# A kernel's own scheduler learns of eight shared transfer places, keeps five input loads under way, and starts the first expert weights later

## The chip, the cores and the metric

The kernel runs on one core of a Trainium2 chip. The core has five engines, each with a queue of instructions of its own that it takes in order: TensorE (PE; its weight loads are shown apart as PEld), VectorE (DVE), ScalarE (ACT), GpSimd (POOL) and SyncE (SP), which here only issues transfers. Transfers are issued by SP, ACT and POOL and carried by 16 DMA engines. The metric is the device time of one execution in microseconds, and less is better; the median over runs counts.

## The reference

Decayed causal attention without a softmax (a retention layer) over 8 batches, 8 heads, 576 positions and a head size of 64, and then a mixture of 8 experts over the 4608 rows of 512 that come out of it. Each row goes to the two experts with the highest noisy logits.

```python
def _attn_ref(q, k, v):
    scores = np.matmul(q, k.transpose(0, 1, 3, 2)) / np.sqrt(D_)
    gamma = 1.0 - 2.0 ** (-5.0 - np.arange(H))
    Dmat = np.where(rel >= 0, gamma[:, None, None] ** rel, 0.0)     # rel: row - column
    return np.matmul(scores * Dmat, v)

def _moe_ref(x, w_gate, w_noise, noise, w1, w2):
    logits = x @ w_gate + np.log1p(np.exp(x @ w_noise)) * noise
    top2 = np.argpartition(-logits, 2, axis=1)[:, :2]               # and their softmax: top2_w
    for e in range(8):
        for k in range(2):
            mask = top2[:, k] == e
            h = np.maximum(x[mask] @ w1[e], 0.0)                    # 512 to 1024
            out[mask] += top2_w[mask, k, None] * (h @ w2[e])        # 1024 to 512
```

q, k and v are 28.3 MB in float32, the experts' weights 33.6 MB.

## The kernel before

The kernel is written as a list of operations, and a scheduler of its own, `Plan`, decides in which order they are issued. An operation names the engines that may do it with an estimated cost for each, the buffers that it reads and writes, a priority (`prio`, less is sooner) and, where it is a transfer, an estimated transfer time (`dma`). `Plan.run` keeps a model clock: of all operations whose predecessors are placed and whose buffers can be had, it places the one that can start soonest (then the lowest priority), books its engine, and sets its end (`fin`). A transfer ends when its queue's transfer time is through and 2.0 us more have gone (`DMA_LAT`). When all are placed, the instructions are issued in that order. So the estimates make the order of each engine's queue, and no more than that: the waits in the finished program come from the tiles that instructions touch and from the transfers' semaphores. For these the finished program has eight places that the transfers of SP and ACT share, taken in turn in the order of issue, and eight more for those of POOL; a transfer waits until the one that had its place before, eight transfers earlier, has landed. The model of before knows nothing of these places. An `after` argument is a predecessor in the model alone.

What the operations are:

- The attention runs in 16 units (`unit`): four batch pairs, two halves of the heads, two batches each. `load` issues five SP transfers for each unit: k and v in two halves (L390, 0.25 MB each) and q (L385, 0.5 MB), into ten float32 buffers `big`. `load_tail` (L401) brings the last 64 positions of a batch pair in six transfers. `cast` makes bf16 of them: k on ACT or DVE (L420, L422), q and v on DVE or POOL with the decay multiplied in (L428, L435; the tail's on POOL, L578). `tr` transposes K and Q on TensorE (L453), `scores` multiplies them (L478) and DVE evicts with the mask (L486), `states` makes the running state (L509), evicted by L252 (ACT) or L254 (DVE), and `out_` the output (L541 within a chunk, L551 across), evicted into `xT`. `tail` does the same for the tail (L587, L600, L618, L622).
- After each batch pair `route` computes the logits (L652) and a long chain of small DVE and POOL steps on them (L660 to L763), which gives the ranks (L716, L718) and the table of rows (L769, two groups of nine matrix multiplications), and puts the rows back by token (L793), copied to `xr` and stored to `xd` in DRAM by five ACT transfers (L802). The four routings end where the second group of L769 ends.
- `weights` of experts 0, 1 and 2 are cast by POOL transfers, four for each expert: two for w1 (L859) and two for w2 (L863). `record` lets them follow, in the model, the landing of the loads of the units in `WAIT`: 8, 11 and 14. The weights of the experts 3 to 7 come later, by SP into `big` (L873, L876).
- The experts work on tiles of 128 rows in pairs. `fetch` gathers the rows (L913 on POOL, from `xd`), transposes them (L922), `up` multiplies by w1 (L979, 32 for a full pair, in four groups of 8), evicted with the relu (L993, L995), `down` by w2 (L1014, 8 for each tile), and `finish` stores first results to `yd` (L1067 on SP) or adds the earlier result, gathered by L1042, and scatters to `out` (L1075 on POOL). Fifteen tiles, in nine pairs, of the experts 0, 1 and 2 can be done while the attention still runs, as the first three routings close them; all others follow the last routing.

TensorE's queue thus mixes attention, routing and early expert tiles in the order of the model clock until about 202 us, and from there on has expert tiles alone.

Of the kernel before, what the change touches and what calls it, by code (L numbers as in the profile page):

```python
# [27 lines left out]
NH = E * HPE  # L28
FIRST = (1216, 1019, 855, 690, 526, 361, 197, 0)
YOFF = [sum(min(-(-x // P) * P, CAP) for x in FIRST[:e]) for e in range(E + 1)]  # L30
WAIT = (8, 11, 14)
CLOSE = ((256, 0, 0, 0, 0, 0, 0, 0), (512, 384, 384, 0, 0, 0, 0, 0), (768, 640, 512, 0, 0, 0, 0, 0))
PLW = 8
XW = DM // 2 + PLW
# [19 lines left out]
class Plan:  # L54
# [55 lines left out]
    def run(self):  # L110
        free, dma_free = {}, {}
        head = {k: 0 for k in self.fifo}
        used = {}
        ready = [o for o in self.ops if not o.need]
        order = []

        def slot(b, taken):
            s = self.slots[b.cls]
            lim = self.quota[b.cls].get(b.stream, len(s))
            if lim < len(s) and all(head[k] >= len(v) for k, v in self.fifo.items()  # L120
                                    if k[0] == b.cls and k[1] != b.stream):
                lim = len(s)
            if used.get((b.cls, b.stream), 0) + sum(t[1].n for t in taken if t[1].cls == b.cls) + b.n > lim:
                return None
            ok = lambda x: x[1] is None and all(x is not y for t in taken for y in t[0])
            best = None
            for i, x in enumerate(s):
                if b.n == 2:
                    if i % 2 or not (ok(x) and ok(s[i + 1])):
                        continue  # L130
                    c, k = [x, s[i + 1]], (max(x[0], s[i + 1][0]), 0)
                elif not ok(x):
                    continue
                else:
                    c, k = [x], (x[0] + (0.3 if len(s) == 8 and ok(s[i ^ 1]) else 0.0), 1)
                if best is None or k < best[0]:
                    best = k, c
            return best and best[1]

        while ready:  # L140
            pick = None
            for o in ready:
                taken = []
                ok = all(b.cls is None or b.t is not None or b in o.allocs for b in o.bufs)
                if not ok:
                    continue
                for n, b in enumerate(o.allocs):
                    k = (b.cls, b.stream)
                    q = self.fifo[k]
                    m = len([t for t in taken if (t[1].cls, t[1].stream) == k])  # L150
                    if q[head[k] + m] is not b:
                        ok = False
                        break
                    x = slot(b, taken)
                    if x is None:
                        ok = False
                        break
                    taken.append((x, b))
                if not ok:
                    continue  # L160
                t0 = max([y[0] for x, b in taken for y in x], default=0.0)
                best = None
                for e, c in o.eng.items():
                    t = max(t0, free.get(e, 0.0))
                    for p in o.preds:
                        t = max(t, p.fin + (0.0 if p.on == e and not p.dma else self.LAT))
                    x = t + c + (self.BIAS.get(e, 0.0) if len(o.eng) > 1 else 0.0)
                    if best is None or x < best[0]:
                        best = x, e, t, c
                _, e, t, c = best  # L170
                key = (round(t * 20), o.prio, o.i)
                if pick is None or key < pick[0]:
                    pick = (key, o, e, t, c, taken)
            if pick is None:
                raise RuntimeError("no operation can go on: " + str([(o.i, o.prio) for o in ready[:20]]))
            _, o, e, t, c, taken = pick
            ready.remove(o)
            o.on = e
            free[e] = t + c
            o.fin = t + c  # L180
            if o.dma:
                x = max(dma_free.get(e, 0.0), t + c)
                if e == "SP":
                    x += o.dma / 0.95
                else:
                    x += o.dma / 0.5
                    if dma_free.get("SP", 0.0) > t + c:
                        dma_free["SP"] += o.dma
                dma_free[e] = x
                o.fin = dma_free[e] + self.DMA_LAT  # L190
            for x, b in taken:
                for y in x:
                    y[1] = b
                b.t = x[0][2] if b.n == 1 else x[0][3]
                k = (b.cls, b.stream)
                head[k] += 1
                used[k] = used.get(k, 0) + b.n
            for b in o.bufs:
                if b.cls is None:
                    continue  # L200
                b.left -= 1
                if not b.left:
                    for x in self.slots[b.cls]:
                        if x[1] is b:
                            x[1] = None
# [12 lines left out]

class Kernel:
# [154 lines left out]
    def unit(u):  # L374
        return u // 4, u // 2 % 2, u % 2

    def load(self, u):
        pl, nc = self.pl, self.nc
        bp, hq, b = self.unit(u)
        d = self.u[u] = {}  # L380
        for n in "kqv":
            t = d["raw" + n] = pl.buf("big", "att")
            s = self.src[n][2 * bp + b, 4 * hq:4 * hq + 4]
            if n == "q":
                pl.op("SP", 0.07, lambda e, s=s, t=t: nc.sync.dma_start(  # L385
                    out=t.t.rearrange("p (h x) -> p h x", h=4), in_=s[:, :512].rearrange("h (p r) d -> p h (r d)", r=4)),
                    w=[t], prio=u, dma=1.6)
            else:
                for c in range(2):
                    pl.op("SP", 0.07, lambda e, s=s, t=t, c=c: nc.sync.dma_start(  # L390
                        out=t.t.rearrange("p (c h x) -> p c h x", c=2, h=4)[:, c],
                        in_=s[:, 256 * c:256 * c + 256].rearrange("h (p r) d -> p h (r d)", r=2)),
                        w=[(t, c)], prio=u, dma=0.96)

    def load_tail(self, bp, prio):
        pl, nc = self.pl, self.nc
        d = self.tails[bp] = {}
        for n in "kqv":
            t = d["raw" + n] = pl.buf("half", "tl")
            for b in range(2):  # L400
                pl.op("SP", 0.07, lambda e, n=n, t=t, b=b: nc.sync.dma_start(  # L401
                    out=t.t[b * HD:(b + 1) * HD].rearrange("p (h d) -> p h d", h=E),
                    in_=self.src[n][2 * bp + b, :, 512:, :].rearrange("h s d -> s h d")),
                    w=[(t, b)], prio=prio, dma=0.8)

    def cast(self, u):
        pl, nc = self.pl, self.nc
# [676 lines left out]

    def record(self):
        pl = self.pl
        self.u, self.tails, self.T, self.xT, self.W, self.t, self.keep, self.scats, self.wdma = {}, {}, {}, {}, {}, {}, {}, {}, []
        self.setup()
        for u in range(3):
            self.load(u)  # L1090
# [39 lines left out]
        for i, t in enumerate(ts[:ne]):  # L1130
# [6 lines left out]
            for fp in range(4):  # L1137
                r, w, c = g.deps(fp)
# [4 lines left out]
        for i in range(ne, len(ts) + 1):  # L1143
# [7 lines left out]
            if i < len(ts):  # L1151
                e = ts[i][0]
# [3 lines left out]
            else:  # L1156
                e, po, hT = ts[-1][0], self.t[i - 1]["po"], self.t[i - 1]["hT"]
# [168 lines left out]
```

## Time and profile before

| | us |
|---|---|
| median of three runs (522.32, 524.5, 525.01) | 524.5 |
| the profiled execution | 519.78 |
| its span, first to last instruction | 518.2 |
| TensorE busy | 435.5 (84%) |
| GpSimd busy | 298.2 (58%) |
| VectorE busy | 222.4 (43%) |
| ScalarE busy | 209.7 (40%) |

The page of the profile cuts the span in 40 equal slices of 13 us and gives the busy share of each in tenths. Here TensorE, the clock that it was granted, and the DMA engines:

```profile
PE   1887639876798899899999889989997799988993
...
PEclk9999757987969579999999999999999799999998
DMA  8999999999765314427679864885865333444333
```

In the first ten slices the DMA engines are full; TensorE is far from full in the first, in the sixth, and by turns up to the sixteenth, where the clock is low in places too. From the seventeenth slice on TensorE is nearly always busy. In these digits a 9 is 90% or more; a busy TensorE is not one at its peak, since multiplications overlap.

Transfers by queue: q1 is SP's, q10 ACT's, q0 POOL's.

```profile
q1 hardware_dynamic: 71874, 60.36, 38.7%
q0 software_dynamic: 15264, 36.89, 26.8%
q10 hardware_dynamic: 4928, 4.87, 2.8%
```

The columns are packets, MB, and the time that the packets took as a share of 16 engines over the span.

### The profile page before, as it was taken

The page shows a single profiled execution, that of the slowest core. Times are in us where ns is not written, and L with a number is a line of the kernel's source. Part 1 is how long each engine was busy: PE and PEld are TensorE (multiplying, and loading weights), DVE is VectorE, ACT ScalarE, POOL GpSimd, SP SyncE. Part 2 cuts the span into 40 slices and gives each one's busy share as a digit, 9 for nine tenths or more (in the row PEclk, how much of TensorE's full clock was granted, in tenths as well). Part 3 has the DMA queues.
Part 4 walks back from the last instruction along what each step waited for, and adds up shares of the span by engine and source line. Part 5 has one row for each costly group of instructions (what it writes and reads, how often), then busy time and mean ns, then how long its engine had stood idle before and what let it go on. Part 6 is the DMA issues. An engine that isn't in the chain of part 4 may idle for free.

```text
span 518.2 us, 12025 instructions
## 1 busy us (share of the span) xinstructions
PE 435.5 (84%) x4784; PEld 296.4 (57%) x4784; DVE 222.4 (43%) x535; ACT 209.7 (40%) x345; POOL 298.2 (58%) x355
## 2 busy tenths in 40 slices
PE   1887639876798899899999889989997799988993
PEld 1665527664576666567565546645645465654661
DVE  2465597793649359411515152341251121312132
ACT  3465425753565454345435334342441222322311
POOL 8846794795677527513253555546447366666453
PEclk9999757987969579999999999999999799999998
DMA  8999999999765314427679864885865333444333
GB/s 242 226 273 231 310 277 267 295 274 294 162 138 99 109 60 143 146 76 246 250 247 372 280 199 134 297 281 162 281 256 175 104 127 120 146 162 132 124 123 104
DMA packets 92125, 102.91 MB, mean 199 GB/s; under 512 B 21502, under 2 KB 70143, under 8 KB 92066
## 3 DMA queue, kind: packets, MB, share of 16 engines
q1 hardware_dynamic: 71874, 60.36, 38.7%
q0 software_dynamic: 15264, 36.89, 26.8%
q10 hardware_dynamic: 4928, 4.87, 2.8%
q8 instruction: 38, 0.62, 0.5%
q14 instruction: 21, 0.17, 0.1%
HBM read 83.20 MB, written 26.63 MB: 212 GB/s over the span
## 4 chain that ended last, share of the span: by engine, by line
PE 46%; issue 15%; POOL 11%; DMA 11%; DVE 7%; SPq 4%; ACT 3%; another core or an unknown queue 1%; POOLq 0%; ACTq 0%; DVEq 0%
PE ps L1014 15%; PE ps L979 14%; DMA xg<-xd,xi 4%; PE ps L509 4%; POOL xg L913 3%; DMA out_dram<-half,xg 3%; POOL half L1042 2%; DMA half<-in_q_dram 2%; PE ps L922 2%; PE ps L453 2%; PE ps L541 2%; PE ps L478 2%; POOL out_dram L1075 2%; SPq L390 2%; DMA big<-in_k_dram 1%
## 5 line engine op out<-in xcount | busy, mean ns | idle before, releaser
L979 PE MATMUL ps<-half,W 128*128 128x256 bf16 (+2 forms) x1344 | 221.2, 264 | 10.2 <-issue 6.1
L1014 PE MATMUL ps<-W,half 128*128 128x512 bf16 x624 | 222.7, 387 | 3.3 <-issue 1.8
L979 PEld LDWEIGHTS <-W 128*128 128x128 bf16 x1344 | 122.4, 98 | 79.9 <-issue 24.1
L993 ACT ACTIVATE half<-ps 128x512 bf16<-128x512 f32 (+2 forms) x160 | 87.1, 558 | 174.2 <-PE ps L979 108.8
L913 POOL DMA_INDIRECT xg<-xd,xi x80 | 83.2, 1040 | 104.9 <-DMA out_dram<-half,xg 24.9
L1014 PEld LDWEIGHTS <-half 128*128 128x128 bf16 x624 | 61.6, 100 | 34.0 <-issue 17.5
L1075 POOL DMA_INDIRECT out_dram<-half,xg x39 | 39.2, 1006 | 33.2 <-DVE half L1071 16.9
L1071 DVE SCALAR_TENSOR_TENSOR half<-ps,xg,half 128x512 f32<-128x512 f32 (+1 forms) x39 | 27.7, 745 | 68.0 <-issue 24.2
L1042 POOL DMA_INDIRECT half<-yd,xg x39 | 39.1, 1002 | 11.9 <-issue 11.6
L486 DVE TENSOR_TENSOR half<-ps,mask 128x512 bf16<-128x512 f32 x64 | 40.2, 708 | 6.5 <-ACT half L1061 3.2
L254 DVE COPY half<-ps 128x1024 bf16<-128x1024 bf16 (+2 forms) x47 | 30.9, 661 | 22.1 <-PE ps L922 8.7
L252 ACT ACTIVATE half<-ps 128x1024 bf16<-128x1024 bf16 (+2 forms) x31 | 29.4, 969 | 24.6 <-POOL oh L763 7.2
L428 POOL TENSOR_TENSOR half<-big,tab 128x1024 bf16<-128x1024 f32 x15 | 29.5, 1964 | 14.8 <-PE ps L551 5.9
L922 PE MATMUL ps<-ident__69,xg 128*128 128x128 bf16 (+1 forms) x320 | 28.7, 225 | 8.7 <-DMA xg<-xd,xi 7.4
L509 PE MATMUL ps<-half,half 64*64 64x64 bf16 (+2 forms) x512 | 32.4, 239 | 2.5 <-issue 1.9
L453 PE MATMUL ps<-ident__69,half 128*128 128x128 bf16 x256 | 24.9, 271 | 9.0 <-ACT half L420 6.0
L922 PEld LDWEIGHTS <-xg 128*128 128x128 bf16 (+1 forms) x320 | 21.4, 102 | 18.2 <-DMA xg<-xd,xi 10.0
L435 POOL TENSOR_TENSOR half<-big,tab 128x512 bf16<-128x512 f32 x26 | 28.4, 1106 | 0.5 <-issue 0.5
L509 PEld LDWEIGHTS <-half 128*64 128x64 bf16 (+1 forms) x512 | 20.1, 117 | 15.0 <-issue 7.2
L252 ACT ACTIVATE tb<-ps 64x512 bf16<-64x512 f32 x30 | 17.7, 591 | 26.4 <-PE ps L509 12.6
L1063 DVE TENSOR_SCALAR half<-ps,xg 128x512 f32<-128x512 f32 x9 | 6.8, 750 | 49.6 <-issue 32.7
L453 PEld LDWEIGHTS <-half 128*128 128x128 bf16 x256 | 21.3, 126 | 10.0 <-ACT half L420 6.0
(173 smaller groups left out, 436.9 us busy)
## 6 DMA issues: line engine op xcount, KB each, us to landing
big<-in_moe_w_dram SPq DMA_DIRECT2D x40, 512.0 KB
yd<-half SPq DMA_DIRECT2D x40, 256.0 KB
big<-in_k_dram SPq DMA_DIRECT2D x32, 256.0 KB
big<-in_q_dram SPq DMA_DIRECT2D x16, 512.0 KB
big<-in_v_dram SPq DMA_DIRECT2D x32, 256.0 KB
W<-in_moe_w_dram POOLq DMA_DIRECT2D x12, 512.0 KB
xd<-xr ACTq DMA_DIRECT2D x16, 264.0 KB
xg<-xd,xi POOLq DMA_INDIRECT x80
```

What stands on the lines that cost most here:

```text
L252: self.nc.scalar.activation(out, in_, Act.Copy)
L254: self.eng(e).tensor_copy(out, in_)
L453: nc.tensor.transpose(v[:, hp, x, :], i[:, y, hp * P:(hp + 1) * P], ident.t)
L486: nc.vector.tensor_tensor(S.t.bitcast(BF16).rearrange("p (h c x) -> p h c x", h=2, c=2)[:, h], p[h].t.rearrange("p (c x) -> p c x", c=2), ...
L509: nc.tensor.matmul(o[h * HD:(h + 1) * HD, hp, n, :], lhsT=kv[0][:k, r, c, 2 * hp + h, :], rhs=m, start=(hp == 0 and c == 0 and k == P and ...
L913: pl.op("POOL", 1.3, lambda _, x=x, h=h, n=n: nc.gpsimd.indirect_dma_start(out=x.t[:n, :], out_offset=None, in_=self.xd[:rows, :], in_offs ...
L922: nc.tensor.transpose(pv()[:, di, s * P:s * P + n], xb[:, di * P:(di + 1) * P], ident.t[:n, :n])
L979: nc.tensor.matmul(pv()[:, f2, :], lhsT=w.t[:, o:o + P], rhs=xv()[:, di, :n], start=(di == 0), stop=(di == KD - 1))
L993: nc.scalar.activation(hv(), pv(), Act.Relu)
L1014: nc.tensor.matmul(po[s].t[:n], lhsT=hv[:, s * P:s * P + n], rhs=w.t[:, o:o + DM], start=(f == 0), stop=(f == KF - 1))
L1042: pl.op("POOL", 1.3, lambda _, b=b, iy=iy, n=self.size(j): nc.gpsimd.indirect_dma_start(out=b.t[:n, :], out_offset=None, in_=self.yd[:rows ...
L1075: ins = nc.gpsimd.indirect_dma_start(out=self.out[:, :], out_offset=IOff(ap=io()[:n], axis=0), in_=o.t[:n, :], in_offset=None, bounds_chec ...
```

## The change

Three things are changed. First, `Plan.run` keeps for each of the two groups of queues (SP and ACT together, POOL) the list of ends of the transfers placed so far, and lets a new transfer start no sooner than the end of the one eight before it. Second, every load of q, k and v, the tails' too, goes through a new function `inp`, which makes it follow, in the model, the fifth load before it, so that five are under way. Third, `WAIT` is (11, 14, 15) instead of (8, 11, 14). No operation is added or taken away; what each computes is the same.

```diff
-WAIT = (8, 11, 14)
+WAIT = (11, 14, 15)
...
         used = {}
+        lanes = {"SP": [], "POOL": []}
+        lanes["ACT"] = lanes["SP"]
...
                     t = max(t0, free.get(e, 0.0))
+                    if o.dma and len(lanes[e]) >= 8:
+                        t = max(t, lanes[e][-8])
...
                 o.fin = dma_free[e] + self.DMA_LAT
+                lanes[e].append(o.fin)
...
+    def inp(self, fn, t, prio, dma):
+
+        self.inps.append(self.pl.op("SP", 0.07, fn, w=[t], prio=prio, dma=dma, after=self.inps[-5:-4]))
+
     def load(self, u):
...
             if n == "q":
-                pl.op("SP", 0.07, lambda e, s=s, t=t: nc.sync.dma_start(
+                self.inp(lambda e, s=s, t=t: nc.sync.dma_start(
...
-                    w=[t], prio=u, dma=1.6)
+                    t, u, 1.6)
...
     def load_tail(self, bp, prio):
...
-                pl.op("SP", 0.07, lambda e, n=n, t=t, b=b: nc.sync.dma_start(
+                self.inp(lambda e, n=n, t=t, b=b: nc.sync.dma_start(
...
-                    w=[(t, b)], prio=prio, dma=0.8)
+                    (t, b), prio, 0.8)
```

The two halves of k and v in `load` are changed in the same way (0.96 each), and `record` starts with an empty list `inps`.

In the finished program the order of all five queues is different. On SP the tails' loads stand later: those of the first batch pair behind unit 4's instead of before unit 3's, those of the second behind unit 8's instead of between unit 6's k and q, those of the third behind unit 12's instead of between unit 10's q and v. On POOL the first w1 transfers of expert 0 stand behind unit 11's casts, those of expert 1 behind unit 14's, and those of expert 2 behind the last L763 of the third routing. On TensorE the first L979 stands behind the second L769 group of the second routing instead of ahead of the first. Some operations that two engines may do change sides: DVE does 4 L254, 3 L422 and 3 L435 less, ACT 4 L252 and 3 L420 more, POOL 3 L435 more. The lines of the changed kernel are 4 to 9 higher than those named here.

More of the change, by code (lines that the diff above doesn't have):

```diff
@@ L384, in load @@
             if n == "q":
-                pl.op("SP", 0.07, lambda e, s=s, t=t: nc.sync.dma_start(
+                self.inp(lambda e, s=s, t=t: nc.sync.dma_start(
                     out=t.t.rearrange("p (h x) -> p h x", h=4), in_=s[:, :512].rearrange("h (p r) d -> p h (r d)", r=4)),
-                    w=[t], prio=u, dma=1.6)
+                    t, u, 1.6)
             else:
                 for c in range(2):
-                    pl.op("SP", 0.07, lambda e, s=s, t=t, c=c: nc.sync.dma_start(
+                    self.inp(lambda e, s=s, t=t, c=c: nc.sync.dma_start(
                         out=t.t.rearrange("p (c h x) -> p c h x", c=2, h=4)[:, c],
                         in_=s[:, 256 * c:256 * c + 256].rearrange("h (p r) d -> p h (r d)", r=2)),
-                        w=[(t, c)], prio=u, dma=0.96)
+                        (t, c), u, 0.96)
     def load_tail(self, bp, prio):
@@ L1086, in record @@
         pl = self.pl
-        self.u, self.tails, self.T, self.xT, self.W, self.t, self.keep, self.scats, self.wdma = {}, {}, {}, {}, {}, {}, {}, {}, []
+        self.u, self.tails, self.T, self.xT, self.W, self.t, self.keep, self.scats, self.wdma, self.inps = {}, {}, {}, {}, {}, {}, {}, {}, [], []
         self.setup()
```

## The prediction

> **What bounds the kernel now.** I read the busy time by stage first, cut at the end of each of the four routings (the second L769 group of each, whose ends the TensorE timeline gives: 75.1, 118.2, 171.3 and 202.4 us); columns are PE, PEld, DVE, ACT, POOL busy, granted clock, DMA share, GB/s:
>
> ```profile
> 0.00:75.10 75.10, 44.91 (x858) 35.17 (x858) 41.93 (x165) 33.80 (x49) 56.51 (x93) 0.88 1.02 261
> 75.10:118.20 43.10, 36.30 (x735) 29.60 (x736) 35.81 (x68) 25.09 (x40) 32.95 (x39) 0.82 1.15 277
> 118.20:171.30 53.10, 40.97 (x736) 31.77 (x738) 32.07 (x68) 27.53 (x44) 35.90 (x46) 0.85 0.79 177
> 171.30:202.40 31.10, 27.56 (x381) 19.53 (x379) 19.11 (x58) 14.56 (x26) 14.85 (x24) 0.75 0.25 81
> 202.40:518.20 315.80, 285.80 (x2091) 180.31 (x2088) 93.50 (x178) 108.75 (x189) 157.94 (x155) 0.98 0.57 188
> ```
>
> TensorE idles 30.2, 6.8, 12.1, 3.5 and 30.0 us in the five stages: 52.6 of 82.6 us before 202.4, where nothing else is full throughout but the DMA engines (1.02 and 1.15). The change does not take a matrix multiplication away, so it can gain only idle time and slow clock; after 202.4 the built order of the changed kernel has the same pattern of gathers and scatters but for a few neighbours exchanged. Second, TensorE's timeline, where the bracket is the idle time and its releaser:
>
> ```profile
> 63.45 0.28 PE L716 MATMUL ps<-MM,ltri 128*128 128x144 bf16 x1 [3.40 <-DVE MM L688]
> ...
> 71.88 0.76 PE L769 MATMUL ps<-oh,olo 128*128 128x80 f16 x9 [5.79 <-POOL oh L763]
> 74.31 0.76 PE L769 MATMUL ps<-oh,olo 128*128 128x80 f16 x9 [1.68 <-POOL oh L763]
> ...
> 115.93 0.78 PE L769 MATMUL ps<-oh,olo 128*128 128x80 f16 x9 [2.58 <-DVE half L486]
> ...
> 122.49 1.07 PE L541 MATMUL ps<-half,half 64*64 64x128 bf16 x32 [3.58 <-ACT tb L252]
> ```
>
> TensorE takes its queue in order, so where a table (L769) stands, it waits for the routing on VectorE and GpSimd. Third, the waits of SP's queue, and ScalarE's wait that lies behind the 3.58:
>
> ```profile
> SPq L401 <- DMA xd<-xr: 7.9, 1, 7.9
> SPq L401 <- DMA half<-in_k_dram: 7.1, 1, 7.1
> ```
> ```profile
> ACT tb L252 <- DMA big<-in_k_dram: 9.7, 1, 9.7
> ```
>
> SP stops 7.9 us at an input load (L401) whose place is held by a store of ScalarE, and ScalarE stops 9.7 us, because its next store of xd holds a place that an input load (the k half issued at 113.73, landing 7.00 us later in the chain of waits) has not left. In the built program each SP or ACT transfer waits for the one eight before it on the two queues together: that is what the old model did not know. Fourth, the queues (packets, MB, share of 16 engines) from 60 to 70 us and then from 70 to 80, and the issues between:
>
> ```profile
> q1 hardware_dynamic: 5150, 3.08, 114.9%
> ```
> ```profile
> q0 software_dynamic: 544, 1.05, 55.8%
> q1 hardware_dynamic: 1609, 0.89, 35.1%
> q10 hardware_dynamic: 705, 0.71, 20.3%
> ```
> ```profile
> 68.26 1.75 POOL L859 DMA_DIRECT2D W<-in_moe_w_dram  x2
> ...
> 72.27 9.14 SPq L401 DMA_DIRECT2D half<-in_q_dram  x2
> ```
>
> When the first weights start, the inputs (q1) fall from 3.08 to 0.89 MB in 10 us.
>
> **The change, part by part.** All prices are against the profiled run, 519.78 us (span 518.2); the median of the three runs, 524.5, lies 4.7 above it, and I add that at the end.
>
> *Tails loaded later.* The built order puts tail 0's six loads behind unit 4 instead of before unit 3, tail 1's behind unit 8 instead of inside unit 6. The timeline has 0.26 + 1.11 + 0.59 = 2.0 us of idle at tail 0 (25.8 to 29.0) and 2.87 at tail 1's first transposition (L587 at 50.78, after GpSimd's L578, which had waited for the q load). Both move behind loads that by then have landed: -4.9. Bounds: 0, if each wait only moves to the next unit, and -4.9.
>
> *Routing 0.* From the last logits (55.57) to the end of the second table (75.07) is 19.5 us, and TensorE idles 0.83 + 3.40 + 5.79 + 1.68 = 11.7 of them, then 1.20 for ScalarE. The new order puts more inside: one unit's scores and states (L478, L509: 0.64 + 1.72), the next unit's scores (0.64), a transposition (L453, 1.07), an L541 and L551 (0.64 + 0.51) and tail 1's L587 (1.03): 6.3 us of work. Against it, VectorE, busy in all of 60 to 80 but 0.7 us, must evict the first unit's scores too: 4 x 0.62 (L486, 2.47 us for four at 77.46) = 2.5. Take 6.3 - 2.5 = -3.8; bounds 0 and -6.3.
>
> *Routing 1.* Expert 0's first 32 L979 (1.03 + 2.95 = 4.0 us) now stand in front of its tables and fill the wait; in the new order they come right behind them. That filler goes: +4.0, less an L541 and L551 (1.15) that now stand between the two tables: +2.9. Bounds 0 (if VectorE is through earlier) and +6.4 (the 10.7 us from rank to table, less 4.3 us of work now left in it).
>
> *Shared places, and weights behind units 11, 14, 15.* The first weights stand behind unit 11's casts on GpSimd, so routing 0's stores meet no weight traffic, and SP's 7.9 us stop goes; routing 1's stores wait for places of loads that SP issued well before. With ScalarE's 9.7 us stop go TensorE's 3.58, and the 1.27 at 129.67 (ScalarE's next evictions, held up behind the same stores at 123.08): -4.9. Of the waits at 134.5 and 138 (1.81 + 1.18, a tail's and a score's) I take none. Bounds 0 and -7.9. If inputs are not late any more, the next thing late is the routing itself, which is counted above.
>
> *Weights late.* Twelve POOL transfers move. One costs GpSimd 0.73 to 0.99 us wherever it stands. The first pair, issued at 68.26 and 69.26, leaves q0 busy to about 80, 11 us. In the new order it stands before routing 1's first L695 on GpSimd, and from that step (100.97) to the end of the second table (118.17) is 17.2 us, so it should land some 5 us before the first L979. Price 0 under that cover; without it each microsecond late is one on TensorE, as the scores of unit 11 are queued behind.
>
> *Engines exchanged.* VectorE loses 4 copies (L254, 0.66), 3 L422 (0.68) and 3 L435 (0.68), 6.7 us in all; ScalarE gains 4 x 0.97 + 3 x 1.07 = 7.1, GpSimd 3 x 1.11 = 3.3. ScalarE is idle 41 of the first 75 us: 0. *The limit of five* is a planner's predecessor alone; the built SP queue waits for places and buffers only: 0, beyond the order already counted.
>
> *Clock.* TensorE busy at a granted 0.53 (60 to 70 us) and 0.50 (70 to 80) is 2.68 and 5.24 us; at 1.00 it would be about 1.4 and 2.6, 3.9 less. As the stop there shortens but does not go, I take half: -2.0; bounds 0 and -3.9. The page "TensorE: Matmul & The Clock Gate" of the Trainium skill (section "HAM oscillation — how this bites in real kernels") says that gaps of more than about 3.4 us bring the half clock; by it the whole 3.9 would come back only if no gap over 3.4 us stays, and the sum would be 1.9 lower; that 20 to 50 us ran at 1.00, with no gap over 2.87, agrees.
>
> Sum: -4.9 - 3.8 + 2.9 - 4.9 - 2.0 = -12.7, so 507.1 for the profiled execution and **512** against the median.
>
> **The rivals.** *The routings set the pace (R1).* From logits to tables took 19.5, 20.4, 21.3 and 15.6 us; VectorE is busy in 35.81 of 43.1 us of stage 2. If these chains, and not the inputs, hold everything, earlier inputs only wait: the tail waits and routing 0's wait only move on, and what stays is the shared places, the lost filler and the clock: -4.9 + 2.9 - 2.0 = -4.0, so 520.5. For it: VectorE saturated at 60 to 80. Against: from 120 to 130 VectorE is busy 2.08, ScalarE 4.49, GpSimd 3.71 us and the DMA share is 1.17.
>
> *Late weights make it slower (R2).* Place: the first L979 behind routing 1's second table. If unit 11's casts reach GpSimd late (they stand behind two gathers of xd rows, and L913 waited 6.25 us there at 85.44), the pair is issued late, and the queue behind it, units 11 to 15, stands. It turns the result when the pair is over 12.7 us late; at 18 us late, -12.7 + 18 = +5.3: 530. For it: GpSimd waits 12.6 us for VectorE's routing steps. Against: the cover of 17.2 us, of which the pair needs 11.
>
> *Nothing is won, for the bytes are the same (R3).* DMA shares of 1.02 and 1.15 could mean that the transfers bound all of it: then 524.5. "DMA: Bandwidth & Descriptors" of the Trainium skill (section "Issuing engines are not separate DMA queues") has all queues share 16 engines; the sums of the shares, 114.9% and 111.2%, agree. Against it stand shares of 0.79 and 0.25 from 118 to 202 us, into which the weights move.
>
> *More than forecast (R4).* All gains at their far ends: -4.9 - 6.3 - 7.9 - 3.9 = -23.0, and +2.9: 504.4.
>
> **How the numbers follow.** Forecast (507 to 517) 0.50, R1 0.20, R2 0.15, R3 0.06, R4 0.09. The sum's own bounds are 524.5 - 23.0 = 501.5 and 524.5 + 6.4 = 531. The range 503 to 524 holds the forecast, R1 and R4 and leaves R2 and half of R3 out, 18%. Under 0.5%, or 2.6 us, a measurement here can't be told from no change: faster means below 521.9. Faster 0.50 + 0.09 + 0.13 of R1 = 0.72; same 0.07 + 0.05 = 0.12; slower 0.15 + 0.01 = 0.16.
>
> **What would show it.** Right: SP's 7.9 us wait for xd and ScalarE's 9.7 us wait for an input gone; q1 at about 300 GB/s up to 100 us, the last inputs issued by about 115 instead of 131; the last table ending near 190; no wait of L979 for weights. Wrong: TensorE idle before the first L979 until a weight lands (R2); tables ending at the old times (R1); or more idle time after the last table than 30 us, since I count nothing there.

## The result, and the profile after

The changed kernel takes 518.8 us (median of 21 runs), the kernel before 523.1 beside it (21 runs). The ratio is 0.9898, 95% interval 0.9874 to 0.9923; like every ratio here, it leaves out runs over 1.5% above the fastest of their kernel. It is faster by 1.0%, some 5.3 us, where 12.7 us had been forecast. Against the 524.5 us that the forecast was made from, this is 519.1: inside the range of 503 to 524, but outside the forecast's own 507 to 517, and nearest to the rival in which the routings set the pace (520.5).

The lines here are from a second profile of the changed kernel (512.38 us, span 510.8; the kernel before beside it 519.8); the first is of a run of 528.2 us. Its lines of code stand up to 9 higher: L778 is the old L769, L988 the old L979, L931 the old L922, L399 and L410 the old L390 and L401. The busy time by stage, divided at the ends of the four routings; columns are PE, PEld, DVE, ACT, POOL busy (instructions), granted clock, DMA share, GB/s:

```profile
0.00:79.00 79.00, 50.43 (x1010) 40.12 (x1012) 45.06 (x168) 42.49 (x59) 61.47 (x93) 0.86 0.98 258
79.00:115.40 36.40, 27.64 (x574) 22.14 (x574) 28.64 (x60) 19.31 (x31) 27.79 (x36) 0.78 1.07 269
115.40:167.20 51.80, 39.34 (x631) 28.96 (x629) 26.71 (x60) 26.87 (x43) 35.48 (x47) 0.87 0.76 162
167.20:201.60 34.40, 26.63 (x508) 20.01 (x508) 23.16 (x64) 18.78 (x35) 18.38 (x29) 1.00 0.67 157
201.60:510.80 309.20, 284.11 (x2069) 179.82 (x2066) 93.85 (x177) 107.06 (x185) 157.95 (x155) 0.97 0.58 191
```

The last table ends at 201.6 us, as before (202.4), not near 190. TensorE's idle time is 28.6, 8.8, 12.5, 7.8 and 25.1 us, 82.7 in all; before it was 82.7 too. Up to the last table it has not fallen but risen, from 52.7 to 57.6 us. The stretch behind, where the forecast counted nothing, is 6.6 us shorter (309.2 instead of 315.8) with 25.1 us idle instead of 30.0: nearly the whole difference of the two spans. Part of it is work brought forward, as 136 of the experts' L988 are done by the last table instead of 120, with 4 more each of L1023 and L931, some 2.8 us in all. The new order also puts other work into the stages, so this division says little of single waits. TensorE's timeline answers to the one shown of before, the bracket again being the idle time and what ended it:

```profile
64.28 0.28 PE L725 MATMUL ps<-MM,ltri 128*128 128x144 bf16 x1 [1.17 <-DVE MM L697]
...
75.79 0.76 PE L778 MATMUL ps<-oh,olo 128*128 128x80 f16 x9 [5.14 <-POOL oh L772]
...
111.62 0.76 PE L778 MATMUL ps<-oh,olo 128*128 128x80 f16 x9 [5.99 <-POOL oh L772]
...
121.60 0.60 PE L988 MATMUL ps<-half,W 128*128 128x256 bf16 x4 [1.42 <-ACT tb L257]
```

In front of routing 0's rank and tables 3.40 + 5.79 + 1.68 us have become 1.17 + 5.14, and none. In front of routing 1's tables 2.58 us have become 5.99: the filler is gone. Behind ScalarE, 3.58 us have become 1.42. The waits of SP's queue (total, times, longest, us):

```profile
SPq L399 <- DMA xd<-xr: 7.4, 2, 7.0
SPq L394 <- DMA xd<-xr: 6.9, 1, 6.9
```

SP's stop at a store of `xd` did not go: there are two of 7 us now, at unit loads, where there was one of 7.9 at a tail load. ScalarE's stop of 9.7 us (`tb` behind an input) is in no list any more. The transfers from 60 to 70 us and from 70 to 80 (packets, MB, share of 16 engines):

```profile
q1 hardware_dynamic: 5280, 2.40, 95.3%
```
```profile
q1 hardware_dynamic: 1911, 1.21, 40.1%
q10 hardware_dynamic: 1232, 1.22, 39.5%
```

With no weights in the way the inputs still fall, to 1.21 MB in 10 us instead of 0.89. ScalarE's stores take as much, and SP stands from 69.5 to 76.6 us at a load whose place one of these stores holds; from 73.0 to 74.2 us the DMA engines are all but empty. From 80 to 100 us q1 moves 3.72 MB (before: 3.60), which is 186 GB/s and not some 300. The last unit's loads leave SP at 118.8 us (before: 117.1), the last tail's at 154.6 (before: 130.7; now the first of them alone waits 17.6 us, for what the profile does not name). The inputs did not come earlier.

The reading that settled most is taken at fixed times. The kernel before, and below it the changed kernel, up to 60, 110, 130, 150 and 200 us:

```profile
0.00:60.00 60.00, 40.71 (x792) 31.61 (x793) 27.42 (x130) 31.69 (x45) 43.09 (x67) 0.97 0.99 252
60.00:110.00 50.00, 35.22 (x722) 28.81 (x718) 42.58 (x96) 25.76 (x41) 38.37 (x56) 0.73 1.15 283
110.00:130.00 20.00, 12.24 (x168) 8.53 (x171) 11.54 (x17) 5.92 (x10) 13.52 (x15) 0.83 1.15 284
130.00:150.00 20.00, 15.83 (x358) 12.32 (x347) 12.42 (x17) 9.96 (x16) 14.54 (x12) 0.90 0.80 164
150.00:200.00 50.00, 43.52 (x634) 32.58 (x633) 32.80 (x94) 26.56 (x45) 28.95 (x49) 0.77 0.37 92
```
```profile
0.00:60.00 60.00, 40.48 (x806) 31.90 (x806) 27.54 (x132) 33.94 (x47) 43.97 (x68) 0.91 1.02 264
60.00:110.00 50.00, 34.18 (x722) 27.48 (x720) 41.44 (x92) 26.41 (x42) 39.89 (x52) 0.78 0.99 252
110.00:130.00 20.00, 14.86 (x328) 12.03 (x328) 15.67 (x26) 9.10 (x14) 15.89 (x18) 0.84 1.00 243
130.00:150.00 20.00, 13.61 (x180) 9.79 (x178) 1.73 (x6) 9.94 (x15) 9.65 (x13) 0.68 0.62 130
150.00:200.00 50.00, 39.32 (x672) 28.79 (x670) 35.77 (x94) 26.66 (x46) 33.06 (x54) 1.00 0.70 153
```

Up to 60 us TensorE idles 19.3 and 19.5 us (the length less PE's busy time): nothing is won where the tails were to give 4.9. From 60 to 110 it is 14.8 and 15.8, from 110 to 130 it is 7.8 and 5.1, and from 130 to 150, 4.2 and 6.4, with VectorE busy for 1.73 us only. Counting the multiplications finished by kind, each at its duration at full clock, gives the work done (an estimate: another price for each kind moves all these sums together by up to 2 us, and the differences by 0.5): by 60 us 32.4 and 32.2 us, by 110 us 64.0 and 63.4, by 130 us 74.2 and 77.8, by 150 us 87.9 and 88.4. So the lead is made between 110 and 130 us, and on this execution most of it is lost in the 20 us behind. By 200 us it is some 4 us again, with the clock (third column from the right) at 1.00 from 150 us on, where the kernel before had 0.77.

### The profile page after: what moved, and what is told of

Same layout as the page of the kernel before. It is cut to its first block, busy times and chain, and to the rows that moved or that the text cites. A ratio compares the mean times of both kernels' runs of the same rounds, so it can differ in the third digit from the quotient of the medians.

```text
span 526.6 us, 11972 instructions
## 1 busy us (share of the span) xinstructions
PE 441.4 (84%) x4741; PEld 300.5 (57%) x4784; DVE 219.6 (42%) x528; ACT 214.4 (41%) x350; POOL 300.7 (57%) x357
## 4 chain that ended last, share of the span: by engine, by line
PE 64%; issue 8%; DMA 8%; DVE 6%; POOL 4%; ACT 3%; SPq 2%; another core or an unknown queue 2%; POOLq 0%; DVEq 0%; ACTq 0%
PE ps L988 25%; PE ps L1023 21%; DMA xg<-xd,xi 5%; PE ps L518 4%; PE ps L931 3%; PE ps L462 2%; PE ps L487 2%; ACT half L257 2%; PE ps L802 2%; PE ps L550 1%; DMA out_dram<-half,xg 1%; SPq L399 1%; PE ps L560 1%; DVE oh L769 1%
## 5 line engine op out<-in xcount | busy, mean ns | idle before, releaser
L988 PE MATMUL ps<-half,W 128*128 128x256 bf16 (+2 forms) x1344 | 228.5, 271 | 14.2 <-issue 5.5
L1023 PE MATMUL ps<-W,half 128*128 128x512 bf16 (+1 forms) x581 | 211.3, 389 | 6.9 <-ACT half L1002 4.1
L988 PEld LDWEIGHTS <-W 128*128 128x128 bf16 x1344 | 124.8, 100 | 90.5 <-issue 34.3
L922 POOL DMA_INDIRECT xg<-xd,xi x80 | 82.1, 1027 | 89.7 <-issue 18.5
L1023 PEld LDWEIGHTS <-half 128*128 128x128 bf16 x624 | 61.8, 100 | 31.9 <-issue 15.8
L1051 POOL DMA_INDIRECT half<-yd,xg x39 | 38.9, 998 | 11.9 <-issue 11.6
L257 ACT ACTIVATE half<-ps 128x1024 bf16<-128x1024 bf16 (+2 forms) x37 | 35.0, 976 | 23.5 <-PE ps L931 7.5
L259 DVE COPY half<-ps 128x1024 bf16<-128x1024 bf16 (+2 forms) x41 | 26.9, 658 | 29.7 <-PE ps L931 18.2
L518 PE MATMUL ps<-half,half 64*64 64x64 bf16 (+2 forms) x512 | 33.9, 242 | 3.8 <-issue 3.8
L444 POOL TENSOR_TENSOR half<-big,tab 128x512 bf16<-128x512 f32 x29 | 31.4, 1101 | 0.0
L931 PE MATMUL ps<-ident__69,xg 128*128 128x128 bf16 (+1 forms) x320 | 27.0, 221 | 5.0 <-DMA xg<-xd,xi 4.2
L257 ACT ACTIVATE xT<-ps 128x512 bf16<-128x512 f32 (+1 forms) x38 | 19.2, 555 | 29.2 <-PE ps L560 10.2
L518 PEld LDWEIGHTS <-half 128*64 128x64 bf16 (+1 forms) x512 | 20.6, 119 | 17.6 <-issue 9.5
L931 PEld LDWEIGHTS <-xg 128*128 128x128 bf16 (+1 forms) x320 | 21.2, 100 | 13.7 <-DMA xg<-xd,xi 5.1
## 6 DMA issues: line engine op xcount, KB each, us to landing
big<-in_moe_w_dram SPq DMA_DIRECT2D x40, 512.0 KB
big<-in_q_dram SPq DMA_DIRECT2D x16, 512.0 KB
W<-in_moe_w_dram POOLq DMA_DIRECT2D x12, 512.0 KB
```

Source lines behind the costliest of these rows:

```text
L257: self.nc.scalar.activation(out, in_, Act.Copy)
L444: self.eng(e).tensor_tensor(o, i, t, Alu.mult)
L518: nc.tensor.matmul(o[h * HD:(h + 1) * HD, hp, n, :], lhsT=kv[0][:k, r, c, 2 * hp + h, :], rhs=m, start=(hp == 0 and c == 0 and k == P and ...
L922: pl.op("POOL", 1.3, lambda _, x=x, h=h, n=n: nc.gpsimd.indirect_dma_start(out=x.t[:n, :], out_offset=None, in_=self.xd[:rows, :], in_offs ...
L931: nc.tensor.transpose(pv()[:, di, s * P:s * P + n], xb[:, di * P:(di + 1) * P], ident.t[:n, :n])
L988: nc.tensor.matmul(pv()[:, f2, :], lhsT=w.t[:, o:o + P], rhs=xv()[:, di, :n], start=(di == 0), stop=(di == KD - 1))
```

## The experiments

Eighteen more runs were made in five sessions (the expectations say "calls"). In three of them (the first and the last two) the kernel before took 520 to 525 us, in the two between 491 us, with the same program. Each ratio is to the runs of the kernel before in its own session, and idle times are compared within one of these two kinds of session only. "Work" is counted as above, and the times are medians.

| kernel | session | us | ratio to before, 95% interval |
|---|---|---|---|
| changed kernel | 1 | 511.9 | 0.987 (0.982 to 0.992) |
| weights behind 11, 14, 15 alone | 1 | 516.6 | 0.992 (0.988 to 0.995) |
| eight places alone | 1 | 527.0 | 1.013 (1.008 to 1.018) |
| change, weights behind 8, 11, 14 | 1 | 520.1 | 1.000 (0.997 to 1.003) |
| change, row of gathers split | 2 | 484.9 | 0.986 (0.981 to 0.992) |
| change, six gathers repeated | 2 | 486.8 | 0.990 (0.986 to 0.994) |
| change without the eight places | 2 | 487.0 | 0.989 (0.983 to 0.995) |
| changed kernel | 3 | 482.8 | 0.985 (0.981 to 0.989) |
| change, row split | 3 | 481.5 | 0.982 (0.978 to 0.986) |
| limit of five alone | 3 | 487.7 | 0.994 (0.992 to 0.997) |
| change, weights behind 9, 14, 15 | 3 | 484.4 | 0.989 (0.985 to 0.992) |
| changed kernel | 4 | 512.0 | 0.982 (0.976 to 0.989) |
| change, tails early again | 4 | 517.3 | 0.994 (0.990 to 0.997) |
| change, noise loads late | 4 | 510.6 | 0.984 (0.980 to 0.988) |
| weights behind 11, 14, 15 alone | 4 | 516.0 | 0.992 (0.988 to 0.996) |
| change, row split | 5 | 517.0 | 0.981 (0.974 to 0.988) |
| change, row split and noise late | 5 | 511.9 | 0.974 (0.969 to 0.979) |

### Which part of the change pays

The first four run the whole change, two parts of it alone, and the change with the weights where they were. The weights alone are this line:

```diff
-WAIT = (8, 11, 14)
+WAIT = (11, 14, 15)
```

The eight places alone are the `lanes` lines of the diff, and the fourth kernel is the whole diff but this line.

> The changed kernel as it is, for a profile that is not disturbed (the first one shows a span of 526.6 us where its median is 518.8). Theory A (inputs starved by weights and by the shared places were the cost, my forecast): the last routing table ends near 191 us, SP's wait of 7.9 us for a store of xd and ScalarE's wait of 9.7 us for an input load are gone, and the missing gain was lost in the stages after it. Theory B (the routing chains on VectorE and GpSimd set the pace): the ends of the four tables stand within 3 us of the old 75, 118, 171 and 202 us, though the inputs are in earlier, and the gain comes from the work that stands ahead of them. Expected time 517 to 519 us.

> The kernel before with WAIT = (11, 14, 15) alone. Theory A: the inputs no longer fall from 3.08 to 0.89 MB per 10 us at 70 us, and at least half of the gain of 5 us is there (under 520.5 where before has 523). Theory B: the inputs come earlier and nothing else does: within 1 us of before, or slower by the 4 us of early expert work that no longer fills the second routing's wait.

> The kernel before with the eight places in the model alone, no limit of five, weights as before. Theory A: ScalarE's 9.7 us wait for an input load goes, but weights still take the DMA engines from 68 us on: a gain of 1 to 3 us. Theory B: the order is another, the pace the same: within 1.5 us of before.

> The changed kernel with WAIT back at (8, 11, 14). Theory A: weights again cut into the inputs, and at least 4 us of the gain go: 522 or more. Theory B: the weights' place does not matter to the pace, and early expert work fills the routings' waits again: 518 or less.

Neither theory of the first expectation came whole: the tables end at 79.0, 115.4, 167.2 and 201.6 us, 0.8 to 4.1 us from the old ends, SP's wait stayed, and the time is under the one expected. The weights alone win 0.8%, and again 0.8% in the fourth session. Their last table ends at 185.5 and 184.8 us, 17 us earlier than before, but with 64 instead of 120 of L988 done by then: an earlier last table is no gain by itself. The eight places alone lose 1.3%, which neither theory had: the order that a model makes out of a truer rule is not by that a better one. With the limit of five on top the loss is gone (1.000 against 1.013), but with the weights early the two together win nothing. Two more kernels complete this: the whole change without the `lanes` lines, and the function `inp` alone.

> The limit of five and the weights behind units 11, 14, 15, without the eight shared places in the model. GpSimd's queue is the same as the changed kernel's up to the fourth routing. If the places in the model are what the gain comes from (theory A, the forecast): 3 to 5 us slower than the changed kernel, ratio about 0.995 to 1.0. If the places are nothing or harmful (alone they cost 1.3%): as fast as the changed kernel or up to 1% faster, ratio 0.98 to 0.988.

> The limit of five alone: the eight places are not in the model and the first weights stay behind units 8, 11, 14. The forecast priced the limit at nothing beyond the order it brings, and put the gain on places and weights: then 0.997 to 1.005. If the order of the inputs is what pays (the limit took the places' loss of 1.3% to 0.0 in an earlier pair): 0.985 to 0.993, as much as the whole change. Idle by 60 us in either case 18 to 20 us, as the transfers are full until then.

Without the places the change wins as much as with them, within the intervals (0.989 against 0.982 to 0.990 in four measurements of the whole): its GpSimd queue is the same up to the last routing. The limit alone wins 0.6%, and 0.992 x 0.994 = 0.986 is what the whole measures. So the gain is that of the weights and of the limit; the places give nothing beside them that these intervals can tell, and beside early weights they seem to cost what the limit wins (1.000 with them, 0.994 without, in two sessions).

> The weights behind units 11, 14, 15 alone, as in the first call. There 0.992 where the kernel before took 520 us. If the parts add up (weights 0.992, limit of five 0.994, product 0.986, the whole change 0.985 to 0.990): 0.989 to 0.995 here.

It came out at 0.992, in the middle. This repeats the weights' part; that the two parts add up rests on the product above, of ratios from different sessions.

### The hole from 126 to 141 us

In the changed kernel's profile of the first session TensorE, VectorE and ScalarE do little from 126 to 141 us (busy 8.1, 3.9 and 3.8 of 15 us), while GpSimd issues eight gathers in a row (L922, 1.0 us each and 0.3 between) with casts behind them. The split moves four of the eight, by a few lines behind the scheduler's loop that rearrange its finished order:

```diff
+        g = [o for o in pool if o.dma == 0.4][6:10]
+        k = pool.index(g[-1])
...
+        k = seq.index(pool[k + 4]) + 1
+        seq[k:k] = g
```

The other kernel issues six of them again at a place where GpSimd idled (`x.fn("POOL")` for each).

> The changed kernel, in whose profile TensorE, VectorE and ScalarE stand nearly still from 126 to 141 us while GpSimd issues eight gathers in a row (1.3 us each) ahead of the v casts of the next unit. Here the last four of the eight, whose rows TensorE first reads at 192 us, go behind those two casts and the pair of weight transfers, into a stretch in which GpSimd idled 7.9 us; nothing else moves. Theory C (the row of gathers makes the hole, by holding up the casts queued behind it and by slowing the hand-overs of the other engines): the hole of some 12 us shrinks by about 5 us, the time falls by 3 to 5 us, 0.6 to 1.0% below the changed kernel. If only the casts behind the row matter, the same; if only the hand-overs matter, half of the hole moves to 141 to 146 us and the time falls by 0 to 2 us. Theory D (the hole has another cause, such as TensorE's own instruction supply): hole and time stay, ratio to the kernel before 0.987 to 0.990.

> The changed kernel with six gathers added, repeats of four of the row into the same buffers with the same rows, behind the last early weight transfer on GpSimd (177.5 us), where GpSimd then idled 10.5 us until VectorE's routing step: 7.8 us of issuing with nothing queued behind it in that time. Theory C in the form that gathers slow the other engines' hand-overs: TensorE, ScalarE and VectorE stand still for some 4 to 8 us more between 178 and 190 us and the time rises by 3 to 6 us (0.6 to 1.2%). If the row only harms by what is queued behind it: no change, under 0.3%. Theory D: no change either.

> The changed kernel once more, beside the next three on one chip. Expected ratio to the kernel before 0.986 to 0.991. For the account of its gain (tails loaded later worth nothing, since by 60 us every profiled execution so far has idled 17.9 to 20.3 us and done 32 us of matrix work; routing 0 -4, routing 1 +3.5, ScalarE's stop -3.5 to -6): the same gaps again, idle by 60 us 18 to 20 us, the wait in front of routing 1's tables 6.0 us, in front of routing 0's 5.2 us. If the hole from 126 to 141 us belongs to the kernel: it is here again. If it belongs to the chip it ran on: only where the kernel before, too, takes about 520 us.

> The changed kernel with the last four of the eight gathers behind the casts and the weight pair, beside the changed kernel itself. Theory C (the row of gathers makes the hole): 3 to 5 us faster than the changed kernel where that shows the hole, and no hole here; no change where it shows none. Theory D (the hole belongs to the chip or the execution): within 0.3% of the changed kernel on every chip, and hole or no hole alike in both.

> The changed kernel with the last four of the eight gathers behind the casts and the weight pair, a third time. Where the kernel before takes about 520 us, the changed kernel idles 6.4 to 6.7 us in gaps of 1 us and more between 126 and 141 us and has done 88 to 91 us of work by 150 us (ratio 0.982 and 0.987 in two calls). Theory C (the row makes the hole there): gaps of at most 2 us in that stretch, 93 us or more by 150 us, ratio 0.972 to 0.980. Theory D (whatever makes such calls slow makes the hole, row or no row): gaps of 5 us or more, 88 to 91 us, ratio 0.980 to 0.988. Where the kernel before takes about 490 us: no hole, 93 to 96 us, ratio 0.980 to 0.987 by both.

In the third session, where the kernel before took 491 us, the changed kernel has its row of eight and no hole: from 125 to 143 us TensorE is busy 15.2 us, against 10.5 in the first session and 11.7 in the fourth. The row alone doesn't make it; and as the ratio is 0.985 without the hole and 0.987 and 0.982 with it, the hole does not seem to be what the gain lacks. What differs is how soon an engine goes on when another is done. In the first session's profile, ScalarE's first two evictions of rows behind L802 (ended 129.5 and 130.5):

```profile
129.46 1.01 PE L802 MATMUL ps<-ident__69,xT 128*128 128x128 bf16 x8
```
```profile
133.46 1.02 ACT L257 ACTIVATE xr<-ps 128x1024 bf16<-128x1024 bf16 x1 [4.44 <-PE ps L518]
137.02 1.02 ACT L257 ACTIVATE xr<-ps 128x1024 bf16<-128x1024 bf16 x1 [2.54 <-issue]
```

and in the third session's:

```profile
126.56 0.61 PE L802 MATMUL ps<-ident__69,xT 128*128 128x128 bf16 x8
```
```profile
126.66 1.94 ACT L257 ACTIVATE xr<-ps 128x1024 bf16<-128x1024 bf16 x2 [0.42 <-PE ps L802]
```

There they follow at once, here 4.0 and 6.5 us after the multiplication that they wait for. (The first bracket names L518, the last to end before the wait did; the program is the same, and its wait is for L802, as the third session's line has it.) The split in a session of the longer kind (the fifth) shortens the stop, and TensorE is busy 13.8 of those 18 us instead of 10.5 and 11.7:

```profile
134.49 1.94 ACT L266 ACTIVATE xr<-ps 128x1024 bf16<-128x1024 bf16 x2 [3.14 <-PE ps L527]
```

Its gaps of 1 us and more from 126 to 141 add to 1.5 us instead of 6.5 and 5.9, as theory C expected, but its work by 150 us is 88.8 us, as theory D did, and its ratio of 0.981 cannot be told from the changed kernel's. Over the five sessions the split is at 0.981, 0.982 and 0.986 and the changed kernel at 0.982, 0.985, 0.987 and 0.990: if it wins, then about 0.3%. The six extra gathers cost nothing that their interval can tell (0.990), but they ran in a session without the hole, so they do not test the other kind. So theory C holds for the gap and not for the time, and why hand-overs are late in such sessions stays open.

### Where the early terms went

The first weights early and the others late put some of routing 1's lost filler back:

> The changed kernel with the first expert's weights behind unit 9 and the other two left behind 14 and 15. In its order 16 matrix multiplications of the first expert (2 us) and 24 transpositions of gathered rows (2.4 us) stand in front of routing 1's tables again, which in the changed kernel wait 6.0 us. If the filler lost there is a real price of the change (forecast +2.9, measured +3.4 to +3.6 in idle time): 2 to 4 us faster than the changed kernel, ratio 0.980 to 0.986. If the early weight traffic takes back as much from the inputs, as it did with all three pairs early (1.0): 0.990 to 1.0.

The wait in front of routing 1's tables fell from 6.0 us to 1.5, and by 110 us 64.9 us of work were done instead of 63.4. At 156 us a new wait of 4.8 us stands where the changed kernel of that session has none, and the ratio is 0.989 against 0.985: the filler's price is real at its place, but in this execution as much is lost elsewhere.

> The changed kernel beside the next three, as their measure: ratio to the kernel before 0.985 to 0.990.

> The whole change, but tail 0's six loads stand in front of unit 3's again, as in the kernel before, and tail 1's in front of unit 8's. By the forecast's first term: 4.9 us slower than the changed kernel (1.0%), with idle places in front of tail 0's and tail 1's transpositions. If full transfers set the pace until 60 us: the same time within 0.4%, the same idle time and work at 50 to 60 us, with the idle time in other places.

> The whole change, but the four noise loads (wanted only by routing 0, at 60 us) stand behind unit 4's loads, not in front of unit 1's and unit 2's; the orders of TensorE and GpSimd stay the same up to the third routing. If the gain at the tails is there and the noise loads take it back: idle time by 60 us 2 us lower and the time 2 to 4 us lower (0.4 to 0.8%). If full transfers set the pace: the second unit starts 1 to 2 us earlier, idle time and work at 60 us are the same, and the time is within 0.4% of the changed kernel.

The tails are put back by recording `load_tail` ahead of `load(u + 3)` (at u = 0 and 5), so that the chain of five has them there; the noise loads are recorded behind unit 3's with `after` on its last load. The changed kernel of that session idles 19.4 us by 60 us. With the tails early, and below with the noise late:

```profile
0.00:60.00 60.00, 40.77 (x840) 31.88 (x842) 29.16 (x139) 34.97 (x50) 44.92 (x71) 1.00 0.98 254
```
```profile
0.00:60.00 60.00, 39.51 (x866) 30.84 (x866) 30.95 (x138) 35.57 (x49) 44.77 (x70) 0.99 1.01 266
60.00:110.00 50.00, 32.53 (x668) 26.28 (x665) 41.52 (x89) 24.45 (x38) 40.52 (x51) 0.74 0.99 257
```

Tails early: idle 19.2 us, and work 33.1 against 32.2 at a clock of 1.00 against 0.91. The tails' place is worth nothing here: 16.2 us are idle by 30 us against 15.2, and by 40 us both have idled 17. The kernel is 1.1% slower, about what the forecast's first term asks for, but not by that term. The loss comes later: up to 110 us it has done the same 63.4 us of work, by 130 us it is 2.1 behind and by 200 us 4.4, with 96 instead of 136 of the experts' L988 done by its last table, as the scheduler also moved weights and expert tiles. Noise late: the second unit starts at 20.6 us instead of 22.5, and by 30 us TensorE has idled 13.2 us instead of 15.2; but by 60 us it is 20.5 against 19.4. That 2.3 us more work is done by then goes with the clock, 0.99 against 0.91. From 60 to 110 us it idles 17.5 us (50 less 32.53) instead of 17.0, and at 110 us the work is 63.5 against 63.4. What an earlier start wins is waited away behind it.

> The kernel before, once more, for a second profile. If the difference of the two kernels lies in the granted clock and not in idle time, as the first two profiles have it (TensorE idle 82.7 us in both, busy 435.5 against 428.2): idle time again 82 to 84 us, and the clock from 171 to 202 us again near 0.75. If that clock was an accident of one execution: near 1.0 there, and a span near 512 us.

The second profile of the kernel before (494.8 us, TensorE idle 70.7) fell in a session of the other kind, so it answers neither number; it did show the wait behind ScalarE again (5.0 + 2.6 us from 119 to 133).

> The split row and the noise loads behind unit 4, in one kernel. If both help: 0.5% or more below split_third. If routings and inputs set the pace up to 110 us, so that an earlier start only waits there: within 0.4% of split_third.

With both edits the kernel has the lowest ratio of all, 0.974 (0.969 to 0.979). It is 0.7% below the split alone by the ratios of that session (medians 511.9 against 517.0), though the intervals overlap, and the late noise alone had won nothing (0.984 against 0.982). It beats the kernel before by 2.6%; that it beats the changed kernel is likely and not shown in one session.

## Why the prediction was wrong

- **Tails loaded later, -4.9: the step that failed.** It said that both waits "move behind loads that by then have landed". The waits did go, and others of the same sum came: idle by 60 us is 19.3 before and 19.5, 19.4 us after, 17.9 and 20.2 in the sessions of the other kind, and 19.2 with the tails early again. In all these executions the DMA engines' share up to 60 us is 0.97 to 1.02. Shown is that this sum does not follow the tails' place. That the full transfers are the reason fits the share, but no run here took bytes out of that stretch to test it. The forecast had that share on the table and used it only for rival R3. Beside it the new order put the noise loads ahead of unit 1, which was not priced: 2 us at the start, won back by the run with the noise late and lost again by 60 us.
- **Idle time in front of the last table, -10.7 in sum (all terms but the clock): not there.** It is 52.7 us before and 57.6 and 53.3 in the changed kernel's profiles of the first and fourth sessions, with some 2.8 us more expert work done; in the other kind, 51.2 and 47.9. Of the rise, the hole holds most (6.5 us of gaps from 126 to 141 us, where the kernel before has 2.5), though the ratio is no better in the session without it. Behind the last table, where the forecast counted nothing, it fell from 30.0 to 25.1 and 22.8, and in the other kind from 19.5 to 14.8. Why it fell there no run here shows.
- **Routing 0, -3.8, and routing 1, +2.9: right.** Gaps of 1 us and more at routing 0 went from 12.1 us to 7.5 (-4.6), at routing 1 from 4.4 to 7.9 (+3.5); in the other kind of session 11.6 to 7.2 and 4.9 to 8.0.
- **Shared places and weights, -4.9: right in size at its place, wrong in cause.** Behind ScalarE 4.9 us became 1.4 in the first session, 7.6 became 1.0 in the other kind (-3.5 and -6.6), the gaps of the hole not counted. But SP's stop did not go and doubled. And ScalarE's stop of 9.7 us is missing in the profiles of each part alone too: of the weights, of the limit, and of the places, with which the kernel loses 1.3%. That a stop goes is not yet a gain.
- **Clock, -2.0: one execution can't tell.** The time at half clock was 75.3 us before, and 67.7, 80.4 and 47.8 in three executions of the changed kernel. TensorE's busy time fell 7.4 us with idle time unchanged in the first, and 1.5 with 6.4 us less idle time in the second. The forecast leaned on long gaps as the cause. In the stretch from 22.9 to 54.1 us of the first execution no gap is longer than 1.2 us, and yet:

```profile
22.90:43.80 20.90, 17.52 (x399) 13.44 (x395) 10.44 (x19) 13.43 (x20) 13.32 (x12) 1.00 1.07 274
43.80:54.10 10.30, 9.55 (x159) 7.74 (x157) 4.87 (x8) 6.92 (x9) 7.96 (x7) 0.50 1.14 310
```

  The clock is 0.50 for 10.3 us in which TensorE is busy 9.55. By the rule of the page "TensorE: Matmul & The Clock Gate" of the Trainium skill (section "HAM oscillation — how this bites in real kernels"), that a kernel should have no idle gaps over some 3.4 us, it should have stayed whole. Here the measurement differs, and decides: long gaps alone do not set the clock.
- **Weights late, 0: right.** No L988 waits for a weight in the profile; R2's wait didn't come.
- **The limit of five, 0 beyond the order: not priced as a part.** Alone it wins 0.6%, by the order it brings.

Without the tails' term the sum is -12.7 + 4.9 = -7.8, or 516.7 us. The four measurements of the ratio (0.982 to 0.990) are -9.3 to -5.3 us of 524.5, so in size what is left of the sum would do. That it does is in part luck, as the idle time in front of the last table did not fall by it. R1 came nearest in time. Its earlier inputs did not come with the change, so they were not tested by it; for R1 speaks that by 110 us every profiled kernel, whatever its order, has done 61.8 to 65.6 us of work, and that the earlier start with the noise late was waited away. It was wrong in that routing 0's wait did shrink.

## What to carry to other kernels

Read idle time and work done at fixed times in both profiles before crediting a wait that is gone: here, up to 60 us, the waits that went came back elsewhere with the same sum. Price each part of a scheduler change by the order that it makes, not by the truth of its rule: the truest part here cost 1.3% alone. A term of 2 us for the clock can't be read from single executions whose time at half clock varies by 30 us.

## What the runs showed of the hardware

The same program took 491 us in two sessions and 520 to 525 in three, some of them on the same chip. In the profiles of the longer sessions hand-overs between engines seem to come late at places. Of 466 semaphore updates of TensorE in the first session's profile of the changed kernel, some 60 are recorded over 0.8 us after the end of the multiplication, up to 5 us and more; in the third session's, none of 465. For ScalarE it is 44 of 333 against 1. But records are also lost there: 443 are found where TensorE's 466 are due, and 286 of ScalarE's 333, so ScalarE's 44 may all be lost ones. The stops behind L802 above are in the timeline itself. At 355 us of that profile TensorE, ScalarE and VectorE all stand for 2.5 us, beside a gather that GpSimd issues. Each of the ten kernels of the first, fourth and fifth sessions has such a stop of 2.2 to 2.6 us between 349 and 367 us, and none of those of the second and third has one of even 1 us from 300 to 420. The first profile of the kernel before, 518.2 us long, has none of even 1 us between 349 and 367 us either, so the stop does not come with every long time.
